# Order of matmuls at two places of a transformer block: wide matmuls of the MLP's second product in rows of five, and one fill behind the transposes

## The chip, the core and the metric

The kernel runs on one core of a Trainium2 chip. The core has a matrix engine (PE in the profile, with PEld for its weight loads), a vector engine (DVE), a scalar engine (ACT), a general engine (POOL) and a queue engine (SP) that issues transfers. Each works through its own list of instructions in order and waits for the others by semaphores. The metric is the device time of one execution in microseconds (us), as the median of several runs. A span is the time from the first to the last instruction in one profiled execution.

## The reference

One block over 2048 tokens of width 512: linear attention with a learned feature map, then an MLP that mixes over the tokens.

```python
h  = x + _A_ref(_layernorm(x), wqkv, w_phi, wo)
h2 = h + _B_ref(_layernorm(h), w1, b1, w2, b2)

# _A_ref: 32 heads of width 16
q, k, v = split(x @ wqkv)
pq, pk = q @ w_phi, k @ w_phi                       # per head
phi_q = concat(softmax(pq), softmax(-pq)); phi_k likewise
o = phi_q (phi_k^T v) / (phi_q sum(phi_k) + 1e-6)
return o @ wo

# _B_ref: tokens S = 2048, hidden F = 1792, channels D = 512
u = gelu(einsum("bsd,sf->bdf", layernorm(x), w1) + b1)
y = einsum("bdf,fs->bds", u, w2) + b2
return y.transpose(0, 2, 1)
```

## The kernel before

Every fp32 product is made from two parts: a value is split into a high part (`hi`, fp32r) and the rest (`lo`), and hi·hi + hi·lo + lo·hi is summed in PSUM. `mm3` (L63) issues these three matmuls, on lines L65, L66 and L67, each with 512 columns.

**Attention.** Tokens go in 16 tiles of 128. After the projections of keys and values comes a loop of 20 iterations (L648) that runs as a pipeline with an order written out by hand for PE, DVE, ACT and POOL: what the code issues first runs first on its engine. One iteration `it` works on several tiles at once:

- `s_pq(it+1)` (L465, POOL) weights a tile's query features `eq`, and `s_ez(it+3)` (L447, POOL) makes the products for a later tile's denominator.
- `s_tr(it)` (L526) transposes tile `it`'s features on PE: eight matmuls on L532 into the PSUM tile `tn`. ACT copies `tn` out in two halves (`pht`, L534). There is one buffer of `tn`, so the next user of it waits for the second copy.
- In even iterations `s_num` (L543) multiplies two tiles' transposed features with the key-value matrix (32 small matmuls on L551, into `tn` again), which ACT (L557) and DVE (L562) take out.
- `s_wo(it-2)` (L564) is the output projection, twelve matmuls into `po`; `s_h` (L575) adds the residual on DVE.
- `s_hn(it-4)` (L592) makes the normalised tile `hs` for the MLP, its high part on ACT (L60) and its low part on POOL (L61).
- `fill(p)` (L627) is a piece of the MLP's first product: for the pair `p` of 128-column blocks of `w1` and the next tile `hs` it issues two `mm3`, six matmuls, into `pu`. The weight operands are columns of `w1` (`whi`, `wlo`), streamed through SP, ACT (L614) and DVE (L606). Two of the seven pairs are filled inside the attention loop; `fills(it)` (L642) issues for pair 1 the tile `it-6` and for pair 0 the tile `it-5`. The tile for pair 0 is the one whose `hs` the iteration before has made.

**First product.** The other five pairs follow back to back (L755), with the activation and the preparation of the operands of the second product between them.

**Second product.** It is done by blocks of 2×2 with seven products in place of eight. The token pair `sp` (0 to 7) is the outer loop and the hidden pair `p` (0 to 6) the inner one; a pair (`sp`, `p`) is a step. The seven weight operands of a step, 128×128 each, come from `w2` through SP, DVE (L785 to L787, L805) and ACT (L796) in groups of two steps; the seven moving operands `UB[p, b]` (tiles `un` and `uf`, 128×512: 256 columns of the high part and 256 of the low) stay in memory. The table `PROD` gives a step's order: weight operand, moving operand, PSUM bank (six banks, `py`), and half.

- Five of the products are wide: one matmul of the high weights over all 512 columns (L823), so that hi·hi comes into the first half of the bank and hi·lo into the second, and then one of the low weights over 256 columns into the first half (L824). I call these W and N.
- Two products share a bank and are narrow: three matmuls of 256 columns each into their half (L827).

The last token pair (`LAST`) has narrow products only. Each step issues the seven products one after another; the last two steps of a token pair are run together (`run_on`), a bank at a time, so that the banks are finished one by one and DVE and ACT take them out while PE goes on.

Of the kernel before, what the change touches and what calls it, by code (L numbers as in the profile page):

```python
# [22 lines left out]
NP = NF // 2  # L23
# [5 lines left out]
V_NOT = (0, 1, 11)  # L29
SUMS = 8  # L30
LAG = 5
WARM = 9
EPS = 1e-5

# [2 lines left out]
def block_kernel(ctx: ExitStack, tc: tile.TileContext, x, xT, wT, phic, wo, w1, b1, w2, b2,  # L37
                 kvmask, ident_in, out):
    nc = tc.nc
# [486 lines left out]
    def s_tr(t):  # L526
        j, i = divmod(t, 2)
        if i == 0:
            PHT[j] = ak.tile([P, NG, 2, P], F32, name="pht", bufs=1)
        ptr = ps_t.tile([P, 2, 4, P], F32, name="tn")  # L530
        for g in range(NG):
            nc.tensor.transpose(ptr[:, g // 4, g % 4, :], EQ[t][:, g, :], ident)  # L532
        for half in range(2):
            nc.scalar.activation(PHT[j][:, half * 4:half * 4 + 4, i, :], ptr[:, half], AF.Copy)  # L534
# [92 lines left out]
    def fill(p, pool=None):  # L627

        t = FN[p]
        FN[p] = t + 1  # L630
        if FL[p] <= t:
            fill_load(p)
        if any(part is WI[p, t - t % 2][1] for part, _, _ in LATER):
            flush()
        if t == 0:
            PU[p] = [pool.tile([P, D], F32, name="pu", tag="pu") for _ in range(2)]
        a, b = WI[p, t - t % 2]
        for c in range(2):
            mm3(PU[p][c], a[:, t % 2, c * P:(c + 1) * P], b[:, t % 2, c * P:(c + 1) * P],
                HN[t][:, 0], HN[t][:, 1], t == 0, t == NT - 1)  # L640

    def fills(it):  # L642
        if FN[1] < it - LAG:
            fill(1, ps_q)
        if FN[0] <= it - LAG:
            fill(0, ps_f)

    for it in range(NT + 4):  # L648
        even = it % 2 == 0
        if 0 <= it + 1 < NT:  # L650
            s_pq(it + 1)
        if it == 0:
            s_tr(0)
            s_kv()
        if it == 1:
            run(q_logits(0))
            q_mm()
            s_tr(1)
        if it > 1 and even and it <= NT:
            s_num(it // 2 - 1)  # L660
        den = s_den(it + 2) if it + 2 < NT else []
        if it > 1 and even and it <= NT:
            ol = s_ol(it // 2 - 1)
            run(ol[:1] + den[:1] + ol[1:])
            den = den[1:]
        if it < NT:
            s_x(it)
        if it + 3 < NT:
            s_ez(it + 3)
        negate()  # L670
        q_mm()
        fills(it)
        q_exp(0)
        logits = q_logits(1)
        if it >= 4 and even:
            s_hn(it - 4)
        if 3 <= it < NT + 3 and even:
            s_moments(it - 3)
        if it > 1 and even and it - 2 < NT:
            s_wo(it - 2)  # L680
        if 1 < it < NT:
            s_tr(it)
        if it > 1 and not even and it - 2 < NT:
            s_wo(it - 2)
        if it >= 4 and not even:
            s_hn(it - 4)
        if 3 <= it < NT + 3 and not even:
            s_moments(it - 3)
        if 3 <= it < NT + 3:
            s_rstd(it - 3)  # L690
        run(logits + (q_sums(0) if it > 0 else []), den)
        if it > 0:
            negate()
        if not logits:
            flush()
        if 0 <= it - 2 < NT:
            s_h(it - 2)
        flush()
        for p in range(2):
            if it >= LAG - 3 + p and FL[p] <= FN[p] + 2 * (FN[p] > 0):  # L700
                fill_load(p)
# [116 lines left out]
            (4, 3, 5, None))  # L818
    LAST = ((2, 1, 0, 0), (5, 5, 0, 1), (0, 0, 1, 0), (1, 4, 1, 1), (3, 6, 2, 0), (6, 2, 2, 1), (4, 3, 3, 0))

    def product(o, half, a, b, first, start, stop):
        if half is None:
            nc.tensor.matmul(o, a[0], b, start=start, stop=stop, skip_group_check=True)  # L823
            nc.tensor.matmul(o[:, 0], a[1], b[:, 0], start=False, stop=stop, skip_group_check=True)  # L824
            return
        for i, (x, y) in enumerate(((0, 0), (0, 1), (1, 0))):
            nc.tensor.matmul(o[:, half], a[x], b[:, y], start=start and first and i == 0, stop=stop and i == 2,  # L827
                             skip_group_check=True)

    def products(sp, ps, order):  # L830
        for a, b, bk, half in order:
            for p in ps:
                wh_, wl_ = AW[sp, p]
                product(bank[bk], half, (wh_[:, a], wl_[:, a]), UB[p, b], half != 1, p == 0, p == NP - 1)

    def flat(a):
        return a.rearrange("p k d -> p (k d)")
# [3 lines left out]
    for n, (sp, p) in enumerate(STEPS):  # L841
        t = 2 * sp
        last = t + 2 == NT
        if n % GRP == 0 and p < NP - 1:
            lo_w2()
            hi_w2()
            sums_w2()
        if p == 0:
            bank = []
            for _ in range(6):  # L850
                pool = (ps_f, ps_q, ps_b, ps_b)[n_bank % 8 // 2]
                bank.append(pool.tile([P, 2, HD], F32, name="py", tag="pu"))
                n_bank += 1
        order = LAST if last else PROD
        run_on = 3 if last else 2
        if p < NP - run_on:
            products(sp, [p], order)
            continue
        if p < NP - 1:
            continue  # L860
        products(sp, range(NP - run_on, NP), order)
        e = uo.tile([P, 2, HD], F32, name="e")
        u2 = uo.tile([P, HD], F32, name="u2", bufs=1)
        u3 = uo.tile([P, HD], F32, name="u3")
        if not last:
            ot = uo.tile([P, 2, 2, HD], F32, name="ot", bufs=1)
            low = uo.tile([P, 3, HD], F32, name="low", bufs=1)
            nc.scalar.activation(e[:, 1], bank[0][:, 0], AF.Copy)
            for i in range(3):
                nc.scalar.activation(low[:, i], bank[3 + i][:, 1], AF.Copy)  # L870
            nc.vector.tensor_add(e[:, 1], bank[0][:, 1], e[:, 1])
            nc.vector.tensor_sub(u2, bank[1][:, 0], e[:, 1])
            nc.vector.tensor_add(u2, bank[1][:, 1], u2)
            nc.vector.tensor_sub(u3, u2, bank[2][:, 0])
            nc.vector.scalar_tensor_tensor(e[:, 0], bank[2][:, 1], -1.0, u2, op0=ALU.mult, op1=ALU.subtract)

            def out_block(i, h, o, add):
                nc.vector.scalar_tensor_tensor(ot[:, i, h], o, b2s[:, t + i:t + i + 1], add, op0=ALU.add, op1=ALU.add)  # L878

            out_block(0, 0, bank[2][:, 1], u3)  # L880
            out_block(0, 1, bank[3][:, 0], u3)
            nc.gpsimd.dma_start(out[t * P:(t + 1) * P, :], flat(ot[:, 0]), accum_op=ALU.add)  # L882
            if n % GRP == 0:
                lo_w2()
                hi_w2()
            out_block(1, 0, bank[4][:, 0], e[:, 0])
            out_block(1, 1, bank[5][:, 0], e[:, 1])
            nc.gpsimd.dma_start(out[(t + 1) * P:(t + 2) * P, :], flat(ot[:, 1]), accum_op=ALU.add)
            nc.gpsimd.dma_start(out[t * P:(t + 1) * P, HD:D], low[:, 0], accum_op=ALU.add)
            nc.gpsimd.dma_start(out[(t + 1) * P:(t + 2) * P, :], flat(low[:, 1:3]), accum_op=ALU.add)  # L890
            if n % GRP == 0:
                sums_w2()
            continue

        hb = [hp.tile([P, 2, HD], F32, name=f"hb{i}") for i in range(2)]
        for i in range(2):
            nc.sync.dma_start(flat(hb[i]), out[(t + i) * P:(t + i + 1) * P, :])
            nc.vector.tensor_scalar(hb[i], hb[i], b2s[:, t + i:t + i + 1], None, op0=ALU.add)
        nc.scalar.activation(e[:, 1], bank[0][:, 0], AF.Copy)
        nc.vector.tensor_add(hb[1][:, 1], bank[0][:, 0], hb[1][:, 1])  # L900
        nc.vector.tensor_sub(u2, bank[0][:, 1], e[:, 1])
        nc.vector.tensor_sub(hb[1][:, 0], hb[1][:, 0], u2)
        nc.vector.tensor_sub(u3, u2, bank[1][:, 0])
        nc.vector.tensor_add(hb[0], hb[0], u3.unsqueeze(1).to_broadcast([P, 2, HD]))
        nc.vector.tensor_add(hb[0][:, 0], bank[1][:, 1], hb[0][:, 0])
        nc.vector.tensor_sub(hb[1][:, 0], hb[1][:, 0], bank[1][:, 1])
        nc.vector.tensor_add(hb[0][:, 1], bank[2][:, 0], hb[0][:, 1])
        nc.sync.dma_start(out[t * P:(t + 1) * P, :], flat(hb[0]))
        for k, o, q in ((0, bank[2][:, 1], nc.scalar), (1, bank[3][:, 0], nc.sync)):
            nc.vector.tensor_add(hb[1][:, k], o, hb[1][:, k])  # L910
            q.dma_start(out[(t + 1) * P:NT * P, k * HD:(k + 1) * HD], hb[1][:, k])
# [49 lines left out]
```

## Time and profile before

| What | Value |
|---|---|
| Time, median of three runs | 523.97 us (523.72 to 524.6) |
| Time of the profiled execution | 524.12 us |
| Its span | 522.3 us |
| Busy time PE / PEld / DVE / ACT / POOL | 516.6 / 436.5 / 386.5 / 282.3 / 239.8 us |
| Granted PE clock, mean | 0.999 |
| Longest wait of PE for another engine | 1.2 us (for POOL, in the attention loop) |

Times in the views are in us from the start of the span, durations of single instructions in us or ns. A matmul's duration in a row is modelled and overlaps with the next matmul; what a matmul costs is the distance from its start to the start of the next one. "x2" at the end of a row means that two like instructions are merged in it. What stands in square brackets is idle time of the engine ahead of the instruction, and what ended it.

### The profile page before, as it was taken

Reading aid. Unit: us, or ns where it says so; the run is one execution under the profiler, and the core shown is the slowest. Engines: PE = TensorE matmul, PEld = TensorE weight load, DVE = VectorE, ACT = ScalarE, POOL = GpSimd, SP = SyncE. Lnnn points to the kernel's source line nnn. Section 1 sums busy time; section 2 is a strip of 40 time slices with the busy share of each in tenths; the row PEclk is TensorE's granted clock in tenths of the full one; section 3 lists DMA queues with packets and bytes.
Section 4 is the critical chain, followed back from the end, with each engine's and each line's share of the span. In section 5 each row is a group of like instructions: output and inputs, shape, how many; then the busy total and the mean of one; then the engine's idle time right before and its main releaser. Section 6 shows DMA issues by size and latency. Waiting matters only on the chain.

```text
span 522.3 us, 8917 instructions
## 1 busy us (share of the span) xinstructions
PE 516.6 (99%) x3379; PEld 436.5 (84%) x3379; DVE 386.5 (74%) x681; ACT 282.3 (54%) x496; POOL 239.8 (46%) x188
## 2 busy tenths in 40 slices
PE   9999999999999999999999999999999999999997
PEld 8788888887877767888788888888899999999997
DVE  6893999986899998863227424725779888988985
ACT  6999853424246876666956423625453434434430
POOL 2579799985999999874424000000002112212220
PEclk9999999999999999999999999999999999999999
DMA  8544210020131324343333354532215687678734
GB/s 317 198 122 122 80 43 22 1 80 24 30 113 60 102 86 136 105 130 130 102 100 102 102 179 143 176 92 77 76 45 115 158 191 161 120 164 186 163 43 82
DMA packets 36298, 58.52 MB, mean 112 GB/s; under 512 B 3744, under 2 KB 19360, under 8 KB 36256
## 3 DMA queue, kind: packets, MB, share of 16 engines
q1 hardware_dynamic: 31936, 51.37, 31.2%
q0 software_dynamic: 4032, 6.42, 9.1%
q8 instruction: 26, 0.43, 0.3%
q10 hardware_dynamic: 288, 0.17, 0.1%
q14 instruction: 16, 0.13, 0.1%
HBM read 46.81 MB, written 11.14 MB: 111 GB/s over the span
## 4 chain that ended last, share of the span: by engine, by line
PE 90%; POOL 7%; DVE 2%; issue 1%; ACT 0%; POOLq 0%
PE pu L65 12%; PE pu L66 12%; PE pu L67 11%; PE py L823 11%; PE py L827 10%; PE py L824 6%; PE pv L66 3%; PE pv L67 3%; PE pv L65 3%; PE pk_ps L65 2%; PE pk_ps L67 2%; PE pk_ps L66 2%; POOL ez L447 2%; POOL eq L465 2%; PE po L67 2%; PE po L65 2%
## 5 line engine op out<-in xcount | busy, mean ns | idle before, releaser
L66 PE MATMUL pu<-hs,whi 128*128 128x512 f32 x224 | 87.6, 391 | 1.2 <-POOL hs L61 1.2
L65 PE MATMUL pu<-hs,whi 128*128 128x512 f32 x224 | 87.4, 395 | 0.0
L67 PE MATMUL pu<-hs,wlo 128*128 128x512 f32 x224 | 87.0, 389 | 0.0
L606 DVE TENSOR_TENSOR wlo<-wraw,whi 128x512 fp32r<-128x512 f32 x56 | 43.8, 784 | 53.2 <-ACT whi L614 53.0
L882 POOL DMA_DIRECT2D out<-ot x7 | 6.2, 887 | 153.9 <-DVE ot L878 153.9
L796 ACT ACTIVATE whi<-wraw 128x1792 fp32r<-128x1792 f32 x28 | 47.4, 1701 | 46.7 <-PE py L823 20.6
L805 DVE TENSOR_TENSOR wlo<-wraw,whi 128x1792 fp32r<-128x1792 f32 x28 | 56.5, 2022 | 12.1 <-PE py L824 8.9
L823 PE MATMUL py<-uf,whi 128*128 128x512 f32 x175 | 63.4, 399 | 0.0
L614 ACT ACTIVATE whi<-wraw 128x512 fp32r<-128x512 f32 x56 | 34.9, 627 | 49.6 <-PE pu L66 45.3
L65 PEld LDWEIGHTS pu<-hs,whi 128*128 128x128 f32 x224 | 42.1, 188 | 10.9 <-issue 2.5
L66 PEld LDWEIGHTS pu<-hs,whi 128*128 128x128 f32 x224 | 42.1, 188 | 10.4 <-POOL hs L61 2.1
L67 PEld LDWEIGHTS pu<-hs,wlo 128*128 128x128 f32 x224 | 42.1, 188 | 8.6
L824 PE MATMUL py<-uf,wlo 128*128 128x256 f32 x175 | 49.2, 281 | 0.0
L447 POOL TENSOR_TENSOR ez<-eq,zB 128x1024 f32<-128x1024 f32 x16 | 38.4, 2400 | 4.4 <-ACT zB L494 4.4
L827 PE MATMUL py<-uf,whi 128*128 128x256 f32 x210 | 39.0, 283 | 0.0
L823 PEld LDWEIGHTS py<-uf,whi 128*128 128x128 f32 x175 | 33.0, 188 | 6.8
L200 POOL TENSOR_TENSOR pk<-pk,sk 128x1024 f32<-128x1024 f32 x16 | 31.0, 1940 | 7.6 <-DVE sk L199 5.0
L534 ACT ACTIVATE pht<-tn 128x512 f32<-128x512 f32 x32 | 17.4, 596 | 30.2 <-PE tn L532 30.2
L827 PEld LDWEIGHTS py<-uf,whi 128*128 128x128 f32 x210 | 32.4, 189 | 1.4
L824 PEld LDWEIGHTS py<-uf,wlo 128*128 128x128 f32 x175 | 33.1, 189 | 0.0
L465 POOL TENSOR_TENSOR eq<-eq,w 128x1024 f32<-128x1024 f32 x16 | 32.3, 2017 | 1.3 <-DVE w L462 1.2
L61 POOL TENSOR_TENSOR hs<-hn,hs 128x512 fp32r<-128x512 f32 x16 | 21.6, 1350 | 23.7 <-ACT hs L60 23.7
(179 smaller groups left out, 1344.2 us busy)
## 6 DMA issues: line engine op xcount, KB each, us to landing
wraw<-in_w SPq DMA_DIRECT2D x56, 256.0 KB, 2.8
wraw<-in_w SPq DMA_DIRECT2D x28, 512.0 KB, 4.1
xraw<-in_xT SPq DMA_DIRECT2D x16, 256.0 KB, 2.8
xh<-in_x SPq DMA_DIRECT2D x16, 256.0 KB, 2.6
h<-in_x SPq DMA_DIRECT2D x16, 256.0 KB, 2.7
out<-h SPq DMA_DIRECT2D x16, 256.0 KB, 2.4
out<-ot POOLq DMA_DIRECT2D x14, 256.0 KB, 4.8
wraw<-in_wT SPq DMA_DIRECT2D x12, 256.0 KB, 4.4
```

The costliest lines, as they stand in the source:

```text
L65: nc.tensor.matmul(o, ah, bh, start=first, stop=False)
L66: nc.tensor.matmul(o, ah, bl, start=False, stop=False)
L67: nc.tensor.matmul(o, al, bh, start=False, stop=last)
L447: nc.gpsimd.tensor_mul(EZ[t], EQ[t], zB)
L465: nc.gpsimd.tensor_mul(heads(EQ[t]), heads(EQ[t]), W[t].rearrange("p g c h -> p (g c h)").unsqueeze(2).to_broadcast([P, 2 * H, DH]))
L606: LO.append(nc.vector.tensor_sub(wl_, raw, wh_).ins)
L614: nc.scalar.activation(wh_, raw, AF.Copy)
L796: nc.scalar.activation(WH[g], RAW[g], AF.Copy)
L805: nc.vector.tensor_sub(wl_, RAW[g], WH[g])
L823: nc.tensor.matmul(o, a[0], b, start=start, stop=stop, skip_group_check=True)
L824: nc.tensor.matmul(o[:, 0], a[1], b[:, 0], start=False, stop=stop, skip_group_check=True)
L827: nc.tensor.matmul(o[:, half], a[x], b[:, y], start=start and first and i == 0, stop=stop and i == 2, skip_group_check=True)
```

## The change

It has two parts, which do not touch each other.

**In the ninth iteration of the attention loop** (`it == 9`, an odd one) `fills` issues pair 1 only; the fill of pair 0 is issued later in the iteration, behind `s_tr(9)`. What other engines do, and in which order, stays as it is. The rows below are PE's at this place: `pu_2232` is the end of pair 1's fill with the tile `hs_2351`, `pu_2131` and `pu_2132` are pair 0's fill with the next tile `hs_2424`, `tn` stands for the eight transposes, and `po` is the first matmul of the output projection. Before:

```order
L67 MATMUL pu_2232<-hs_2351,wlo_2300 128x512
L65 MATMUL pu_2131<-hs_2424,whi_2294 128x512
L66 MATMUL pu_2131<-hs_2424,whi_2294 128x512
L67 MATMUL pu_2131<-hs_2424,wlo_2295 128x512
L65 MATMUL pu_2132<-hs_2424,whi_2294 128x512
L66 MATMUL pu_2132<-hs_2424,whi_2294 128x512
L67 MATMUL pu_2132<-hs_2424,wlo_2295 128x512
L532 MATMUL tn_2493<-ident_61,eq_1768 128x128 x8
L65 MATMUL po_2504<-woh_1383,oh_2395 128x512
```

Now, with line numbers one higher:

```order
L68 MATMUL pu_2232<-hs_2351,wlo_2300 128x512
L533 MATMUL tn_2487<-ident_61,eq_1768 128x128 x8
L66 MATMUL pu_2131<-hs_2424,whi_2294 128x512
L67 MATMUL pu_2131<-hs_2424,whi_2294 128x512
L68 MATMUL pu_2131<-hs_2424,wlo_2295 128x512
L66 MATMUL pu_2132<-hs_2424,whi_2294 128x512
L67 MATMUL pu_2132<-hs_2424,whi_2294 128x512
L68 MATMUL pu_2132<-hs_2424,wlo_2295 128x512
L66 MATMUL po_2504<-woh_1383,oh_2395 128x512
```

The transposes have moved ahead of the six matmuls of pair 0's fill; nothing is added or removed.

**In the second product** a new function `step` takes the place of `products` for the steps with `p` from 1 to 4 of the token pairs 0 to 6 (28 steps): it issues the five W of the step first, then the five N, then the two narrow products. Steps with `p == 0` stay as they were. In the two steps that are run together (`p` 5 and 6) a bank gets W, W, N, N in place of W, N, W, N. The last token pair has no wide products, and its order is the same. The rows below are one step of PE, `p == 2` of one token pair (`py_4647` to `py_4652` are its six banks). Before, in pairs of W and N (the first four banks of the step):

```order
L823 MATMUL py_4647<-uf_3993,whi_4561 128x512
L824 MATMUL py_4647<-uf_3993,wlo_4633 128x256
L823 MATMUL py_4648<-uf_4003,whi_4561 128x512
L824 MATMUL py_4648<-uf_4003,wlo_4633 128x256
L827 MATMUL py_4649<-uf_3993,whi_4561 128x256 x2
L827 MATMUL py_4649<-uf_3993,wlo_4633 128x256
L827 MATMUL py_4649<-uf_4003,whi_4561 128x256 x2
L827 MATMUL py_4649<-uf_4003,wlo_4633 128x256
L823 MATMUL py_4650<-uf_4008,whi_4561 128x512
L824 MATMUL py_4650<-uf_4008,wlo_4633 128x256
```

Now (W and N stand on one line, L841, and the narrow products on L845), the step up to the first narrow product, behind which the second one ends it:

```order
L841 MATMUL py_4647<-uf_3993,whi_4561 128x512
L841 MATMUL py_4648<-uf_4003,whi_4561 128x512
L841 MATMUL py_4650<-uf_4008,whi_4561 128x512
L841 MATMUL py_4651<-uf_3998,whi_4561 128x512
L841 MATMUL py_4652<-uf_3998,whi_4561 128x512
L841 MATMUL py_4647<-uf_3993,wlo_4633 128x256
L841 MATMUL py_4648<-uf_4003,wlo_4633 128x256
L841 MATMUL py_4650<-uf_4008,wlo_4633 128x256
L841 MATMUL py_4651<-uf_3998,wlo_4633 128x256
L841 MATMUL py_4652<-uf_3998,wlo_4633 128x256
L845 MATMUL py_4649<-uf_3993,whi_4561 128x256 x2
L845 MATMUL py_4649<-uf_3993,wlo_4633 128x256
```

The W stand in a row of five over five banks, the N in another, and the six narrow matmuls have gone to the end of the step. The count of each kind is the same.

The diff:

```diff
+BEHIND = 9

-    def fills(it):
+    def fills(it, both):
         if FN[1] < it - LAG:
             fill(1, ps_q)
+        if both:
+            fill_last(it)
+
+    def fill_last(it):
         if FN[0] <= it - LAG:
             fill(0, ps_f)

-        fills(it)
+        fills(it, it != BEHIND)
...
         if 1 < it < NT:
             s_tr(it)
+        if it == BEHIND:
+            fill_last(it)

-    def product(o, half, a, b, first, start, stop):
-        if half is None:
-            nc.tensor.matmul(o, a[0], b, start=start, stop=stop, skip_group_check=True)
-            nc.tensor.matmul(o[:, 0], a[1], b[:, 0], start=False, stop=stop, skip_group_check=True)
-            return
-        for i, (x, y) in enumerate(((0, 0), (0, 1), (1, 0))):
-            nc.tensor.matmul(o[:, half], a[x], b[:, y], start=start and first and i == 0, stop=stop and i == 2,
-                             skip_group_check=True)
-
     def products(sp, ps, order):
         for a, b, bk, half in order:
-            for p in ps:
-                wh_, wl_ = AW[sp, p]
-                product(bank[bk], half, (wh_[:, a], wl_[:, a]), UB[p, b], half != 1, p == 0, p == NP - 1)
+            if half is None:
+                for low in range(2):
+                    for p in ps:
+                        wide(sp, p, a, b, bk, low)
+            else:
+                for p in ps:
+                    narrow(sp, p, a, b, bk, half)
+
+    def wide(sp, p, a, b, bk, low):
+        w, u = AW[sp, p][low][:, a], UB[p, b]
+        o, u = (bank[bk][:, 0], u[:, 0]) if low else (bank[bk], u)
+        nc.tensor.matmul(o, w, u, start=p == 0 and not low, stop=p == NP - 1, skip_group_check=True)
+
+    def narrow(sp, p, a, b, bk, half):
+        for i, (x, y) in enumerate(((0, 0), (0, 1), (1, 0))):
+            nc.tensor.matmul(bank[bk][:, half], AW[sp, p][x][:, a], UB[p, b][:, y], start=p == 0 and half == 0 and i == 0,
+                             stop=p == NP - 1 and i == 2, skip_group_check=True)
+
+    def step(sp, p, order):
+        for low in range(2):
+            for a, b, bk, half in order:
+                if half is None:
+                    wide(sp, p, a, b, bk, low)
+        for a, b, bk, half in order:
+            if half is not None:
+                narrow(sp, p, a, b, bk, half)

         order = LAST if last else PROD
         run_on = 3 if last else 2
+        if p == 0:
+            products(sp, [p], order)
+            continue
         if p < NP - run_on:
-            products(sp, [p], order)
+            step(sp, p, order)
             continue
```

## The prediction

> **What bounds the kernel now.** I read the page first, then the waits of PE, then stretches of time, and then two places in the timeline. The page's first and second parts:
>
> ```profile
> PE 516.6 (99%) x3379; PEld 436.5 (84%) x3379; DVE 386.5 (74%) x681; ACT 282.3 (54%) x496; POOL 239.8 (46%) x188
> ...
> PE   9999999999999999999999999999999999999997
> ...
> PEclk9999999999999999999999999999999999999999
> ```
>
> PE is busy all the time at full granted clock, so what PE issues, and the distance at which it issues, is the time. All that PE waits for elsewhere is in one short list (the waits of PE; columns: total us, times, longest us):
>
> ```profile
> PE pu L66 <- POOL hs L61: 1.2, 1, 1.2
> PE pk_ps L293 <- DVE eps L56: 1.1, 1, 1.1
> PE pk_ps L129 <- ACT wkh L285: 0.2, 1, 0.2
> ```
>
> The second and third lie in the start. The first is a fill that waits for the low part of a normalised tile. Where it lies shows a table by stretch (PE busy, PEld, DVE, ACT, POOL, clock):
>
> ```profile
> 184.00:196.00 12.00, 10.84 (x83) 8.16 (x82) 10.56 (x22) 8.90 (x20) 11.51 (x9) 1.00 0.31 95
> 196.00:250.00 54.00, 54.00 (x379) 43.06 (x377) 35.51 (x76) 37.74 (x84) 39.62 (x27) 1.00 0.39 123
> ```
>
> From 184 to 196 us PE misses 1.16 of 12 us and POOL is nearly full; from 196 to 250 PE misses nothing and POOL has 14 us of room. So in the ninth iteration POOL is late and PE waits for it; behind that place PE paces.
>
> **Part 1: pair 0's fill behind the transposes.** PE's timeline there, and the rows of ACT and POOL that it meets:
>
> ```profile
> 186.68 0.39 PE L67 MATMUL pu<-hs,wlo 128*128 128x512 f32 x1
> 186.91 0.39 PE L65 MATMUL pu<-hs,whi 128*128 128x512 f32 x1
> 188.46 0.50 PE L66 MATMUL pu<-hs,whi 128*128 128x512 f32 x1 [1.16 <-POOL hs L61]
> 188.80 0.40 PE L67 MATMUL pu<-hs,wlo 128*128 128x512 f32 x1
> ...
> 189.74 1.03 PE L532 MATMUL tn<-ident,eq 128*128 128x128 f32 x8
> 190.53 0.48 PE L65 MATMUL po<-woh,oh 128*128 128x512 f32 x1
> 190.84 0.40 PE L66 MATMUL po<-wol,oh 128*128 128x512 f32 x1
> ```
> ```profile
> 185.73 1.09 ACT L534 ACTIVATE pht<-tn 128x512 f32<-128x512 f32 x2 [1.02 <-PE tn L532]
> ...
> 187.74 1.15 ACT L176 ACTIVATE eq<-eq,r 128x1024 f32<-128x1024 f32 x1
> 190.81 1.09 ACT L534 ACTIVATE pht<-tn 128x512 f32<-128x512 f32 x2 [1.92 <-PE tn L532]
> ```
> ```profile
> 182.44 1.94 POOL L465 TENSOR_TENSOR eq<-eq,w 128x1024 f32<-128x1024 f32 x1
> ...
> 186.69 1.72 POOL L61 TENSOR_TENSOR hs<-hn,hs 128x512 fp32r<-128x512 f32 x1
> ```
>
> Pair 0's fill starts at 186.91, and its second matmul, the first to need the low part, waits until POOL's L61 is through at 188.41. The transposes follow at 189.74 and take 0.79 us (to 190.53). Now they come first. They need three things: the features from POOL's L465 (done at 184.38), the `tn` buffer, which is free when ACT's second copy of the tile before ends at 186.82, and PE itself, free at 186.91. So they run from 186.91 to 187.70, and all of it lies in what was the wait. The fill's first matmul goes at 187.70, the second is ready some 0.31 us later (190.53 to 190.84 is what that first distance behind transposes takes) at 188.01, and waits to the same 188.46. From there the five matmuls run as before to 189.74, and the output projection starts then in place of 190.53: 0.79 us gained. The long first distance behind transposes (0.31 against 0.23 us) has also gone into the wait: 0.08 more. Gain 0.87 us. A wait of about 0.3 us is left over (188.46 less the end of a 0.48 us matmul from 187.70).
>
> POOL's L61 itself does not move: it follows on POOL without a gap and waits for no transposes. No transfer, and no instruction of another queue, is moved. Behind the moved matmuls on PE stands the output projection, which only gets earlier. ACT's copies of the transposes, which waited 1.92 us, can now start behind its exponential at 188.89 in place of 190.81; with them the next tile's `hs` gets its high part earlier.
>
> Does the gain last? PE's next need of POOL is the same wait one iteration on:
>
> ```profile
> 193.67 1.81 POOL L61 TENSOR_TENSOR hs<-hn,hs 128x512 fp32r<-128x512 f32 x1 [0.49 <-ACT hs L60]
> ...
> 207.62 1.29 POOL L61 TENSOR_TENSOR hs<-hn,hs 128x512 fp32r<-128x512 f32 x1 [0.83 <-ACT hs L60]
> ```
> ```profile
> 196.22 0.39 PE L66 MATMUL pu<-hs,whi 128*128 128x512 f32 x1
> ```
>
> Before, the low part was done at 195.48 and wanted at 196.22. Now it is wanted at 195.35. Since ACT is earlier, POOL's 0.49 us of idle time goes, L61 ends near 195.0, and PE doesn't wait. If POOL did not get earlier, PE would lose 0.13 us and a slow restart of 0.11 us (188.46 to 188.80 against 0.23), and the gain would be 0.63. That is the lower end; nothing excludes more gain up to the whole wait, 188.46 less 187.14, 1.32 us. I take 0.87. From 207 us on POOL waits for ACT and not the other way, so nothing further back takes it away.
>
> **Part 2: rows of five.** The price of a matmul is the distance between starts. One step before (token pair 2, `p` 3), PE's timeline:
>
> ```profile
> 421.73 0.40 PE L823 MATMUL py<-uf,whi 128*128 128x512 f32 x1
> 421.96 0.28 PE L824 MATMUL py<-uf,wlo 128*128 128x256 f32 x1
> 422.08 0.40 PE L823 MATMUL py<-uf,whi 128*128 128x512 f32 x1
> 422.32 0.28 PE L824 MATMUL py<-uf,wlo 128*128 128x256 f32 x1
> 422.44 0.40 PE L827 MATMUL py<-uf,whi 128*128 128x256 f32 x2
> ...
> 423.16 0.40 PE L823 MATMUL py<-uf,whi 128*128 128x512 f32 x1
> ...
> 424.22 0.40 PE L823 MATMUL py<-uf,whi 128*128 128x512 f32 x1
> ```
>
> A W with the N behind it takes 0.354 us: two from 421.73 to 422.44 and three from 423.16 to 424.22 are 1.77 us, by five. The six narrow matmuls take 0.72 us, 0.120 each. Of the pair, N to W is 0.12 (421.96 to 422.08; 0.118 fits the sum) and W to N 0.236. What W to W costs isn't to be seen in this stage; the nearest row is the first product, where matmuls of the same 512 columns stand in a row (eighteen from the first to the last of these):
>
> ```profile
> 299.92 0.39 PE L65 MATMUL pu<-hs,whi 128*128 128x512 f32 x1
> 300.15 0.39 PE L66 MATMUL pu<-hs,whi 128*128 128x512 f32 x1
> ...
> 303.78 0.39 PE L67 MATMUL pu<-hs,wlo 128*128 128x512 f32 x1
> ```
>
> Seventeen distances in 3.86 us are 0.227 each, 0.009 less than W to N. So a change of width costs, and the step had five such pairs. The step now: four W to W at 0.227, one W to N at 0.236, five N at 0.120 like the narrow ones, the six narrow ones at 0.72 as before. Five wide products cost 0.908 + 0.236 + 0.600 = 1.744 in place of 1.770 us: 0.026 gained a step, 0.73 us in 28 steps. In the two steps run together, W, W, N, N costs 0.227 + 0.236 + 0.120 + 0.118 = 0.701 in place of 0.708: 0.007 for each of 5 banks of 7 token pairs, 0.25 us. Together 0.98 us, all on PE and so on the path.
>
> Bounds: if W to W costs 0.236 like W to N, the step's wide products take 5 × 0.236 + 0.600 = 1.78, a loss of 0.01, and the quads 0.710, a loss of 0.002: 0.35 us lost. If a row takes the best of all rows, 0.227 after every W and 0.117 after every N, the step gains 0.05 and the quads 0.02: 2.1 us. I take the values of the rows with the same columns and loads, 0.98.
>
> A rule of the Trainium skill speaks against this part: its page "TensorE: Matmul & The Clock Gate", section "Back-to-back issue gap", gives the distance of matmuls by a matmul's own number of columns. By it order is free, and the part would bring 0 in place of 0.98 us. The trace differs: with 512 columns each, 0.236 us with a narrow one behind and 0.227 with a wide one.
>
> What else moves: within a step the narrow products' operands are wanted later, and the last wide product's earlier, by at most a step's length of 2.5 us. The last moving operands to be made are these, and they are first used at 391.9 us (the seventh step; six steps of 2.49 us behind the first step's start at 379.48):
>
> ```profile
> 382.76 1.09 DVE L61 TENSOR_TENSOR uf<-tt,uf 128x256 fp32r<-128x256 f32 x3
> ```
> ```profile
> 379.48 0.39 PE L823 MATMUL py<-un,whi 128*128 128x512 f32 x1
> ```
>
> The operands are done at 383.85; the cover is 8 us. The weights' low part is wanted at the sixth matmul of a step and not at the second, so DVE has more room. The weights' buffers and the banks come free as before, in the last matmuls of a step and bank by bank. DVE is busy here but waits for PE, and PE waits for nobody:
>
> ```profile
> 379.40:501.00 121.60, 121.60 (x785) 110.19 (x784) 107.44 (x164) 51.63 (x59) 21.06 (x24) 1.00 0.63 141
> ```
>
> DVE has 14 of 122 us left, and the stage gets 1 us shorter, so its cover stays.
>
> **The sum.** 0.87 + 0.98 = 1.85 us. The profiled execution took 524.12 us (span 522.3 and 1.8 around it), so 522.27; it stands 0.15 above the median of 523.97, and against that the time is 522.1 us, 0.35% less. What this kernel's measurement can tell from no change is about 0.2%, 1.05 us, so each part alone lies within it and both together beyond.
>
> **Rivals.**
>
> *The rows bring nothing.* The 0.009 us may belong to this stage (weights cut out of larger tiles, a bank per product) and not to the change of width. Then only part 1 is left: 523.97 − 0.87 = 523.1 us. For it: no W to W stands in this stage. Against it: the six narrow matmuls here cost 0.120 each with the same weights, as flat as the first product's rows. The rule of the Trainium skill named above would come out here too.
>
> *The wait comes back.* POOL is full until 196 us; if the next L61 ends later than 195.3, or the transposes wait for ACT's copy longer than until 187.4 (when the wait no longer hides them), part 1 shrinks towards 0 and part 2 alone gives 523.0 us. Against it: the idle times of POOL at 193.67 and 207.62, and 0.5 us of cover for the transposes.
>
> *Rows of N are dear (the slower side).* A weight load has 0.188 us in the profile, and an N gives its successor only 0.12 us to load behind:
>
> ```profile
> L824 PEld LDWEIGHTS py<-uf,wlo 128*128 128x128 f32 x175 | 33.1, 189 | 0.0
> ```
>
> Between W the loads had a long matmul beside them; in a row of five N they have not. Should each N of a row cost 0.188 us, that is 0.068 more for 28 × 5 and for 35 more of the quads: 11.9 us, and the time 534.0. From 0.131 us an N (1.85 by 175 above 0.120) the whole gain is lost, and from 0.137 the kernel is over 0.2% slower. Against it: the narrow products, which load six times in a row at the same width, keep 0.120 us. They use only three pairs of weights and one bank, five N use five of each, so it isn't excluded.
>
> **How the numbers follow.** Both parts as worked out: 0.77, at 522.1 us, its own range 521.6 to 522.7. Rows bring nothing: 0.08, 523.1. The wait comes back: 0.07, 523.0. Rows dear: 0.08, anything from 524.1 to 534. The first case ends beyond the 0.2% nearly always; I give 0.76 to faster, from it. The two middle ones are within 0.2% and make 0.15 with a little of the last, whose rest, with what I don't see, is 0.09 for slower. The range goes from 521.4 (part 2 with half of its upper bound more, 0.5 us, and the scatter of the runs, 0.25 below their median) to 523.2, which takes in both middle cases and leaves out the dear rows.
>
> **What would show it.** PE's wait on POOL's L61 near 188 us should be 0.3 us and the transposes stand ahead of it; the output projection behind them starts at 189.74. Past 196 us PE should have no new wait. A step of the second product should take 2.46 us in place of 2.49, W to W 0.227 and N to N 0.120; the last token pair should be unchanged. The prediction is wrong if W to W here is 0.236, if N to N is over 0.125, or if a second wait on POOL near 195 us takes over the first.

## The result, and the profile after

The changed kernel takes 523.33 us (median of 22 runs, 522.76 to 523.76) against 523.99 us of the kernel before (22 runs, 523.57 to 524.67): ratio 0.9986, 95% interval 0.9980 to 0.9992. So it is 0.66 us faster where 1.85 were forecast, and it lies above the range's upper end of 523.2. The kernel is faster beyond its interval, but by less than the 0.2% that the prediction called the least that can be told.

The profiled execution took 523.76 us with a span of 522.0. First the waits of PE in the changed kernel (total us, times, longest us). The wait that part 1 was to shorten is still 1.2 us:

```profile
PE pu L67 <- POOL hs L62: 1.2, 1, 1.2
PE pk_ps L294 <- DVE eps L57: 1.1, 1, 1.1
PE pk_ps L130 <- ACT wkh L286: 0.2, 1, 0.2
```

PE's timeline of the changed kernel shows why. The wait is where it was, with the transposes still behind the fill. The transposes that have moved ahead of a fill stand 12.6 us later (202.82 against 190.24), and there the second matmul of that fill follows without a wait:

```profile
187.42 0.39 PE L66 MATMUL pu<-hs,whi 128*128 128x512 f32 x1
188.97 0.50 PE L67 MATMUL pu<-hs,whi 128*128 128x512 f32 x1 [1.17 <-POOL hs L62]
...
190.24 1.04 PE L533 MATMUL tn<-ident,eq 128*128 128x128 f32 x8
...
200.56 1.04 PE L533 MATMUL tn<-ident,eq 128*128 128x128 f32 x8
...
202.58 0.39 PE L68 MATMUL pu<-hs,wlo 128*128 128x512 f32 x1
202.82 1.06 PE L533 MATMUL tn<-ident,eq 128*128 128x128 f32 x8
203.64 0.48 PE L66 MATMUL pu<-hs,whi 128*128 128x512 f32 x1
203.95 0.39 PE L67 MATMUL pu<-hs,whi 128*128 128x512 f32 x1
```

The sets of transposes run through the tiles in order. From `it == 9` at 202.82 back, 200.56 is `it == 8` and 190.24 is `it == 7`. The wait belongs to iteration 7, and iteration 9 never had one.

In the second product the steps are shorter. PE's timeline up to the next token pair's `p` 1, first of the kernel before (from token pair 2, `p` 5; its `p` 3 is in the prediction) and then of the changed one (from `p` 3; first W of each step, and the lines between are left out):

```profile
426.70 0.40 PE L823 MATMUL py<-uf,whi 128*128 128x512 f32 x1
...
431.67 0.40 PE L823 MATMUL py<-un,whi 128*128 128x512 f32 x1
...
434.16 0.40 PE L823 MATMUL py<-un,whi 128*128 128x512 f32 x1
```
```profile
421.98 1.32 PE L841 MATMUL py<-uf,whi 128*128 128x512 f32 x5
423.14 0.76 PE L841 MATMUL py<-uf,wlo 128*128 128x256 f32 x5
423.73 0.40 PE L845 MATMUL py<-uf,whi 128*128 128x256 f32 x2
...
424.45 0.40 PE L841 MATMUL py<-uf,whi 128*128 128x512 f32 x1
...
426.93 0.40 PE L841 MATMUL py<-uf,whi 128*128 128x512 f32 x1
...
431.85 0.40 PE L841 MATMUL py<-un,whi 128*128 128x512 f32 x1
...
434.31 0.40 PE L841 MATMUL py<-un,whi 128*128 128x512 f32 x1
```

A step of rows takes 2.47 us (421.98 to 424.45) in place of 2.49. In it five W take 1.16 us, 0.232 each, and five N 0.59, 0.118 each. The two steps run together went from 4.97 to 4.92 us, and the step with `p == 0`, whose order is the same, from 2.49 to 2.46. From the first W to the last matmul the second product took 139.34 us and takes 138.47:

```profile
518.82 0.28 PE L827 MATMUL py<-uf,wlo 128*128 128x256 f32 x1
```
```profile
380.01 0.39 PE L841 MATMUL py<-un,whi 128*128 128x512 f32 x1
...
518.48 0.28 PE L845 MATMUL py<-uf,wlo 128*128 128x256 f32 x1
```

That is 0.87 us less. This execution's second product begins 0.53 us later than that of the profile before, which is no effect of the change: in the first 8 us, ahead of all that is edited, PE got to the second half of the weights' folding at 8.09 here and at 7.53 there, and the matmuls keep that distance up to the loop. In the profiles of the kernels in this document that matmul stands anywhere from 7.14 to 8.09 us.

```profile
7.53 1.95 PE L273 MATMUL pv<-ph,wraw 128*128 128x128 f32 x16
```
```profile
8.09 1.95 PE L274 MATMUL pv<-ph,wraw 128*128 128x128 f32 x16
```

### The profile page after: what moved, and what is told of

It reads as the page before. It is cut to its first block, busy times and chain, and to the rows that moved or that the text cites. A ratio compares the mean times of both kernels' runs of the same rounds, so it can differ in the third digit from the quotient of the medians.

```text
span 522.0 us, 8917 instructions
## 1 busy us (share of the span) xinstructions
PE 516.2 (99%) x3379; PEld 436.7 (84%) x3379; DVE 386.1 (74%) x681; ACT 282.1 (54%) x496; POOL 240.1 (46%) x188
## 4 chain that ended last, share of the span: by engine, by line
PE 90%; POOL 7%; DVE 2%; issue 1%; ACT 0%; POOLq 0%
PE py L841 16%; PE pu L66 12%; PE pu L67 12%; PE pu L68 11%; PE py L845 10%; PE pv L67 3%; PE pv L68 3%; PE pv L66 3%; PE pk_ps L66 2%; PE pk_ps L67 2%; PE pk_ps L68 2%; POOL ez L448 2%; POOL eq L466 2%; PE po L68 2%; PE po L66 2%; PE po L67 2%
## 5 line engine op out<-in xcount | busy, mean ns | idle before, releaser
L841 PE MATMUL py<-uf,whi 128*128 128x512 f32 x175 | 49.8, 395 | 0.0
L448 POOL TENSOR_TENSOR ez<-eq,zB 128x1024 f32<-128x1024 f32 x16 | 38.3, 2399 | 4.4 <-ACT zB L495 4.4
L845 PE MATMUL py<-uf,whi 128*128 128x256 f32 x210 | 39.1, 283 | 0.0
L62 POOL TENSOR_TENSOR hs<-hn,hs 128x512 fp32r<-128x512 f32 x16 | 22.1, 1380 | 23.5 <-ACT hs L61 23.5
L845 PEld LDWEIGHTS py<-uf,whi 128*128 128x128 f32 x210 | 32.8, 192 | 0.0
L841 PEld LDWEIGHTS py<-uf,wlo 128*128 128x128 f32 x175 | 28.6, 189 | 4.9
L205 POOL TENSOR_TENSOR zacc<-zacc,pk 128x1024 f32<-128x1024 f32 x13 | 31.2, 2400 | 0.5
L841 PEld LDWEIGHTS py<-uf,whi 128*128 128x128 f32 x175 | 29.1, 190 | 2.7
```

The costliest lines, as they stand in the source:

```text
L205: nc.gpsimd.tensor_add(zacc, zacc, PK[t])
L448: nc.gpsimd.tensor_mul(EZ[t], EQ[t], zB)
L841: nc.tensor.matmul(o, w, u, start=p == 0 and not low, stop=p == NP - 1, skip_group_check=True)
L845: nc.tensor.matmul(bank[bk][:, half], AW[sp, p][x][:, a], UB[p, b][:, y], start=p == 0 and half == 0 and i == 0, stop=p == NP - 1 and i == ...
```

## The experiments

All times are medians, with the ratio to the kernel before (523.97 us in the first group of four, 523.89 in the second) and its 95% interval.

### Each part alone

**The fill's move in iteration 9 alone.** Against the kernel before:

```diff
+BEHIND = 9
...
-        fills(it)
+        fills(it, it != BEHIND)
...
+        if it == BEHIND:
+            fill_last(it)
```

> Part 1 alone, as in the change: pair 0's fill behind the transposes in iteration 9, the second product as before. Theory (the wait lies in iteration 7, where the transposes of the eighth tile follow the waiting fill, and iteration 9 has none): no change, 524.0 us within 0.2, and PE's wait on POOL's hs stays at 1.2 us. Rival (the move did gain, and the changed kernel's profile hides it behind its 0.5 us later start): 523.1 us, 0.87 less.

Measured: 524.01 us, ratio 0.9999 (0.9990 to 1.0008). The wait on POOL's `hs` is there as before, and from the matmul of the folding (at 7.94 us in this profile) to the first W of the second product (379.88) PE takes 371.94 us, against 371.95 in the kernel before. This part of the change is worth nothing.

**The rows alone.** Against the changed kernel:

```diff
-BEHIND = 9
+BEHIND = -1
```

> Part 2 alone, as in the change: rows of five and quads in the second product, the fill left where it was. Theory (all of the changed kernel's gain is from here): 523.1 to 523.3 us, 0.65 to 0.9 less than before, the second product 0.87 us shorter. Rival (the fill's move had a share): less than 0.5 us gained.

Measured: 522.80 us, ratio 0.9979 (0.9971 to 0.9988). Its second product takes 138.47 us, to the hundredth that of the changed kernel. All of the gain is from here. That the median lies below the changed kernel's is within the intervals; this profile was 0.95 us ahead of the changed kernel's already at the folding (7.14 against 8.09).

### The move at the place of the wait

**In iteration 7, second product as before.** Against the kernel with the move in iteration 9:

```diff
-BEHIND = 9
+BEHIND = 7
```

> The same move of pair 0's fill behind the transposes, but in iteration 7 where the trace of before has the wait; the second product as before. Theory (part 1's working is right and only its place was wrong): the wait falls from 1.2 to 0.3 us, and the time by 0.87 us to 523.1. Rival (POOL is the pace there, and its next hs takes the gain back): a new wait one iteration later, and a gain of 0 to 0.6 us.

Measured: 524.32 us, ratio 1.0009 (1.0001 to 1.0018): no gain, rather a loss. In the profile, level with that of before up to the wait (transposes at 184.66 us in both), the next iteration's transposes come at 200.64 us in place of 200.08. PE's waits in this kernel, but for the shortest:

```profile
PE pu L68 <- DVE wlo L607: 1.2, 1, 1.2
PE pk_ps L294 <- DVE eps L57: 1.1, 1, 1.1
PE pu L67 <- POOL hs L62: 0.2, 1, 0.2
```

The first wait did fall, to 0.2 us where 0.3 was forecast, and the transposes run at 186.92 in the wait's place. But 8 us later PE waits 1.2 us for a low part of the weights, made by DVE:

```profile
186.92 1.06 PE L533 MATMUL tn<-ident,eq 128*128 128x128 f32 x8
187.74 0.48 PE L66 MATMUL pu<-hs,whi 128*128 128x512 f32 x1
188.47 0.50 PE L67 MATMUL pu<-hs,whi 128*128 128x512 f32 x1 [0.24 <-POOL hs L62]
...
193.90 0.40 PE L67 MATMUL pu<-hs,whi 128*128 128x512 f32 x1
195.48 0.51 PE L68 MATMUL pu<-hs,wlo 128*128 128x512 f32 x1 [1.18 <-DVE wlo L607]
```

DVE makes two of these low parts in a row there, and PE wants the second. The rows of DVE and POOL, first of the kernel before (POOL's next, L61 at 193.67, is in the prediction) and then of this one:

```profile
191.50 2.82 DVE L606 TENSOR_TENSOR wlo<-wraw,whi 128x512 fp32r<-128x512 f32 x2
```
```profile
190.77 2.41 POOL L447 TENSOR_TENSOR ez<-eq,zB 128x1024 f32<-128x1024 f32 x1
```
```profile
191.51 3.91 DVE L607 TENSOR_TENSOR wlo<-wraw,whi 128x512 fp32r<-128x512 f32 x2
```
```profile
190.79 2.40 POOL L448 TENSOR_TENSOR ez<-eq,zB 128x1024 f32<-128x1024 f32 x1
193.14 1.73 POOL L62 TENSOR_TENSOR hs<-hn,hs 128x512 fp32r<-128x512 f32 x1
```

DVE starts at the same time but ends at 195.42 in place of 194.32. Such a low part alone takes 0.68 us (46 of the 56 in the kernel before take less than 0.7). The first of the two, beside POOL's L448 (L447 before), takes 2.2 us in both kernels and ends about 0.55 us behind POOL's instruction. Then came the difference: before, POOL stood still for 0.49 us from 193.18 because ACT's high part was late. In that gap, at 193.65, DVE started its second low part, which took 0.68 us, and it was POOL's L61, started at 193.67, that got longer (1.81 us). Now ACT has its high part 2.0 us earlier (at 191.56 in place of 193.59), since the transposes are earlier; POOL goes on at once, at 193.14 (its L62 takes 1.73 us, since DVE's first low part goes on to 193.74), and DVE's second low part takes 1.77 us and ends 0.55 us behind POOL. So what PE had gained it lost again by way of ACT, POOL and DVE.

The Trainium skill has the rule for this, in its page "SBUF — State Buffer", section "SBUF: two separate sides": a DVE operation with two inputs in SBUF and a GpSimd operation that reads it take turns at one pair of ports, and the one that starts second is blocked until the other is through. The trace agrees: 0.68 us alone, 1.77 and 2.2 us behind a POOL instruction. And each of the ten low parts in the kernel before that take over 0.7 us starts while a POOL instruction runs and ends 0.54 or 0.55 us behind that instruction's end.

**The same with the changed kernel's second product.** Against the changed kernel:

```diff
-BEHIND = 9
+BEHIND = 7
```

> The changed kernel with the fill moved in iteration 7 in place of 9. Theory (two independent parts on a PE that is never idle elsewhere): 0.87 + 0.75 us, 522.4 us. Rival (what PE gains early is lost at a later wait): 523.1 or more.

Measured: 523.52 us, ratio 0.9994 (0.9985 to 1.0003). The gain of the rows is there (second product 138.47 us) and the loss in the attention loop too, with the same wait of 1.2 us on DVE's low part. The rival was right.

**The order of two loads turned.** Against the kernel with the move in iteration 7:

```diff
+SWAP = 6
...
-        for p in range(2):
+        for p in (1, 0) if it == SWAP else (0, 1):
             if it >= LAG - 3 + p and FL[p] <= FN[p] + 2 * (FN[p] > 0):
                 fill_load(p)
```

> As the run that moved the fill in iteration 7, and in iteration 6 the two loads of w1 columns are taken in the other order (pair 1 first), so that of the two low parts which DVE makes in a row near 191 us the one that PE wants first comes first. Theory (PE's new wait of 1.2 us came from DVE's second low part, which POOL's hs kept out of memory until it was through): PE finds that low part done at 193.7 us, wanted at 194.1; the wait on DVE is gone, the transposes of the ninth tile come at 199.2 us in place of 200.6, and the time is 0.87 below before, 523.1 us. Rival (DVE is simply behind there by 1.2 us, whichever part comes first): the wait stays, 524.2 us.

Measured: 523.12 us, ratio 0.9984 (0.9975 to 0.9993), the forecast time. DVE's two low parts still take 3.92 us together, but PE finds the first of them done (at 193.66, wanted at 194.08), and its wait on DVE is gone. PE's timeline:

```profile
193.84 0.40 PE L68 MATMUL pu<-hs,whi 128*128 128x512 f32 x1
194.08 0.39 PE L69 MATMUL pu<-hs,wlo 128*128 128x512 f32 x1
...
199.11 1.03 PE L534 MATMUL tn<-ident,eq 128*128 128x128 f32 x8
```

The next iteration's transposes come at 199.11 us, 0.97 earlier than in the profile before (200.08); this profile ran 0.09 ahead at the transposes before the edit, so 0.88 is the edit's. The second product begins 0.97 us earlier as well (378.51 against 379.48): nothing behind the loop takes the gain back. Part 1's sum of 0.87 us was right for the place of the wait, with this second edit to keep it.

### What a W costs

**Rows of two.** Against the rows alone, `step` becomes:

```diff
     def step(sp, p, order):
-        for low in range(2):
-            for a, b, bk, half in order:
-                if half is None:
-                    wide(sp, p, a, b, bk, low)
-        for a, b, bk, half in order:
-            if half is not None:
-                narrow(sp, p, a, b, bk, half)
+        if order is LAST:
+            return products(sp, [p], order)
+        for part in (order[0:2], order[2:4], order[4:6], order[6:7]):
+            for low in range(2):
+                for a, b, bk, half in part:
+                    if half is None:
+                        wide(sp, p, a, b, bk, low)
+            for a, b, bk, half in part:
+                if half is not None:
+                    narrow(sp, p, a, b, bk, half)
```

> Rows of two in place of rows of five: steps with p 1 to 4 issue W W N N, the narrow products, W W N N, W N; the fill is left where it was. Theory (a W costs more for some matmuls behind narrow ones, and W W N N is near its floor, 0.698 us in the changed kernel's quads): a step takes 0.698 + 0.710 + 0.698 + 0.350 = 2.456 us in place of 2.473, 0.48 us less than rows of five, about 522.6 us. Rival (rows of five save by their few changes of width): a step takes 2.48 us or more, 523.5 us.

Measured: 522.71 us, ratio 0.9977 (0.9967 to 0.9987). One step in PE's timeline (W W N N, W N, and the narrow products between):

```profile
401.14 0.62 PE L841 MATMUL py<-uf,whi 128*128 128x512 f32 x2
401.59 0.40 PE L841 MATMUL py<-uf,wlo 128*128 128x256 f32 x2
401.83 0.40 PE L845 MATMUL py<-uf,whi 128*128 128x256 f32 x2
...
402.55 0.63 PE L841 MATMUL py<-uf,whi 128*128 128x512 f32 x2
403.02 0.39 PE L841 MATMUL py<-uf,wlo 128*128 128x256 f32 x2
403.25 0.40 PE L841 MATMUL py<-uf,whi 128*128 128x512 f32 x1
...
403.60 0.62 PE L841 MATMUL py<-uf,whi 128*128 128x512 f32 x2
```

A step takes 2.46 us (401.14 to 403.60) and the second product 137.95 us, 0.52 less than with rows of five and 1.39 less than before. A step has three changes from W to N in place of one, and takes less time: it is not the number of changes that costs. Nor does each W behind narrow matmuls cost the same. The two W behind the six narrow matmuls take 0.47 us (402.55 to 403.02), but the two at the head of the step, right behind the last N of the step before, 0.45 (401.14 to 401.59), no more than in a uniform row. The 0.52 us stand in the profile; the medians of the two kernels, 522.71 and 522.80, don't tell them apart.

**Rows of ten.** Against the rows alone, `step` takes a list of steps and goes through it inside each of its three loops; it is called for `p` 2 and 4:

```diff
-            step(sp, p, order)
+            if last:
+                step(sp, [p], order)
+            elif p % 2 == 0:
+                step(sp, [p - 1, p], order)
```

> Rows of ten: two steps (p 1 and 2, p 3 and 4) issue their ten W, ten N and twelve narrow matmuls together; the fill is left where it was. Theory (the W right behind narrow ones cost more, up to about five of them, then 0.227): the second five W of a row cost 0.227 each, two steps take 4.925 in place of 4.946 us, 0.3 us less than rows of five, about 522.8 us. Rival (a W with other weights and another bank than the one before costs 0.232 in this stage, wherever it stands): the second five W cost 0.232, and the time is that of rows of five, 523.1.

Measured: 527.17 us, ratio 1.0063 (1.0050 to 1.0076), far from both. PE's waits, DVE's low part of the weights, and PE's timeline with one of the waits and a row of ten:

```profile
PE py L841 <- DVE wlo L812: 3.5, 4, 0.9
```
```profile
390.96 2.03 DVE L812 TENSOR_TENSOR wlo<-wraw,whi 128x1792 fp32r<-128x1792 f32 x1 [1.45 <-PE py L845]
```
```profile
391.88 0.28 PE L841 MATMUL py<-uf,wlo 128*128 128x256 f32 x1
393.04 0.39 PE L841 MATMUL py<-uf,wlo 128*128 128x256 f32 x1 [0.89 <-DVE wlo L812]
...
399.94 1.32 PE L841 MATMUL py<-un,whi 128*128 128x512 f32 x5
401.11 1.30 PE L841 MATMUL py<-uf,whi 128*128 128x512 f32 x5
402.24 0.76 PE L841 MATMUL py<-un,wlo 128*128 128x256 f32 x5
402.83 0.76 PE L841 MATMUL py<-uf,wlo 128*128 128x256 f32 x5
403.43 0.40 PE L845 MATMUL py<-un,whi 128*128 128x256 f32 x2
```

The time went into something neither theory had: with ten N in a row and twelve narrow matmuls behind them, both steps' weights are held until the narrow matmuls at the end of the two steps; DVE waits for PE (to 390.96), has the next low part at 392.99, and PE, which wants it at 392.00, goes on at 393.04. In four of the seven token pairs a distance is 1.16 us (391.88 to 393.04) in place of 0.12, over 4 us together. The row itself decides the question. The first five W take 1.16 us in each of the run's fourteen rows, 0.232 each as in rows of five (399.94 to 401.11 in the row shown, where the rounded stamps make it 1.17; 381.56 to 382.72 in the first row). The second five take 1.13 us (401.11 to 402.24), 0.227 each. They have other weights and another bank each as well. So a W in this stage does cost 0.227 us once it is far enough behind narrow matmuls, and in a long row the excess lies in the first five. By these rows two steps take 4.93 us, as the theory said.

### What paid, together

Rows of two in the steps with `p` 0 to 4, the fill's move in iteration 7 and the two loads turned. Against the changed kernel, with `step` as in the run with rows of two:

```diff
-BEHIND = 9
+BEHIND = 7
+SWAP = 6
...
-        if p == 0:
-            products(sp, [p], order)
-            continue
```

> Everything that paid, in one: the fill moved in iteration 7 with the two loads in the other order, and rows of two in all steps with p 0 to 4. Theory (independent parts): 0.87 + 0.87 + 0.5 us below before, 521.7 us. Rival (one of the three doesn't pay, as its own run shows): 522.3 or more.

Measured: 521.87 us, ratio 0.9960 (0.9947 to 0.9972): 2.0 us faster than before, and faster than the changed kernel (523.33). PE's wait on POOL is 0.2 us, and there is none on DVE's low parts:

```profile
PE pu L68 <- POOL hs L63: 0.2, 1, 0.2
```

The rows of two in the step with `p == 0` bring nothing more: this second product takes 138.01 us against 137.95 without them.

## Why the prediction was wrong

**Part 1, the step that failed: "So in the ninth iteration POOL is late and PE waits for it".** The wait lies in iteration 7. The prediction took the place from the order of instructions around the wait (pair 1's fill, pair 0's fill, transposes, output projection), which every odd iteration has, and never counted the sets of transposes up to it. The move in iteration 9 exchanges work where PE never waits: 0 us in place of 0.87, and that is 0.87 of the 1.2 us by which the forecast missed. Part 2 lacks 0.11 us, as worked out below; the rest, some 0.2 us, is less than what the profiles differ by in their first 8 us (7.14 to 8.09).

**"Does the gain last?"** was also answered too quickly. The next need that the prediction looked at was POOL's next `hs`, which does come in time. The one that ends last is DVE's low part of the weights for pair 1, wanted 1.1 us earlier than that `hs`. Its row stood in the trace with 2.82 us for two instructions that take 0.68 each. The prediction counted the end of POOL's idle time only as help; it was also the gap in which DVE got its turn. At the right place, the part alone cost 0.35 us in the median.

What held of part 1: the transposes fit in the wait, nothing else delays them, 0.2 to 0.3 us of the wait are left, and the price is 0.88 us measured against 0.87.

**Part 2, a term that was mis-sized: W to W at 0.227 us.** In a row of five behind narrow matmuls it is 0.232, and the row saves 0.014 us a step in place of 0.026, 0.4 us in 28 steps in place of 0.73. The reason given for it, that a change of width costs, did not hold either: rows of two have more changes and take less time. By luck two other terms made most of it good. The two steps run together gained 0.045 us a token pair (4.970 to 4.925) in place of 0.035, 0.32 us; and the step with `p == 0`, which was taken as unchanged, got 0.026 us shorter in six token pairs, 0.16 us. Its own order is the same, and what goes before it has changed. In the kernel before, the first token pair's step with `p == 0`, which follows the first product, already took 2.46 us (379.48 to 381.94). Together 0.87 us for 0.98 forecast: the sum was near, its parts less so. The price of N in a row (0.118) and the unchanged last token pair were right. The cover of the moving operands was right too, with its place misnamed: 391.9 us is five steps of 2.49 us behind 379.48 and not six, the start of the sixth step, with which the seventh is run together.

**The rivals.** Rows of N being dear fell: 0.118 us. That the rows bring nothing fell too: the second product got 0.87 us shorter. The rule of the Trainium skill (page "TensorE: Matmul & The Clock Gate", section "Back-to-back issue gap") gives the distance by a matmul's number of columns, for a matmul by itself. The trace differs: matmuls of the same 512 columns cost 0.232 and 0.227 us in the two halves of a row of ten. "The wait comes back" was the nearest, with 523.0 us for part 2 alone against 523.33; it named POOL's next `hs` where there were two reasons, a place without a wait and, at the right place, DVE.

**What stays open** is why a W costs more behind narrow matmuls. The runs show where the excess lies in a long row (the first five, whatever the weights and banks), and that two W can be without it right behind an N. So more counts than the matmul just in front; no run takes apart what in PE makes it.

## What to carry to other kernels

A wait in a pipelined loop has to be given its iteration by counting from a landmark in the trace, not by the look of its neighbours, before anything is moved there. When a wait is filled with other work, each engine that gets earlier by it has to be followed to the next thing it shares, over several hand-overs: here a gain of PE went through ACT and POOL to DVE and back. And the distance of two matmuls depends on what ran before them; here a price from a uniform row elsewhere was good to 2% only (0.227 against 0.232 us), more than the 0.6% that the rows gained in a step (0.014 of 2.49 us).

## What the runs showed of the hardware

- A wide matmul (512 columns) cost 0.227 us in a uniform row, and 0.232 us on average in the first five of a row behind narrow ones (256 columns); a single W between N cost 0.236 on average in the kernel before. The excess was gone after five, as the row of ten shows.
- The same sequence of matmuls can cost different times by what stood before it: the unchanged step with `p == 0` went from 2.49 to 2.46 us, and W W N N took 0.69 us at the head of a step in the rows of two (401.14 to 401.83) but 0.70 behind the narrow products (402.55 to 403.25).
- A DVE subtraction of 0.68 us took 1.77 and 2.2 us when it had started beside a running POOL instruction, with its end 0.55 us behind POOL's; in the other order POOL's took 1.81 in place of 1.29 us.
